# Zero fills in the plan, another order of first loads, V stores by token and three new constants in a kernel whose whole instruction order is planned ahead

## The chip, the cores and the metric

The kernel runs on one core of a Trainium2 chip. The metric is the device time of one execution in microseconds (us), median of several runs. The profile's span is about 1.8 us shorter than the time of the same execution, so spans are compared with spans and times with times.

PE is the matmul engine, DVE the vector engine, ACT the scalar engine, POOL is GpSimd, and SP is the engine that issues most transfers.

## The reference

Two rounds of an attention layer with a recurrent memory, each followed by a gated feed-forward layer, on x of 1 x 2048 x 512 in bf16. What matters is the recurrence: the 2048 tokens go through the attention in 64 segments of 32, and each needs the 8 memory rows that the one before has made.

```python
def _A_ref(x, mem0, Wq, Wk, Wv, Wo, seg_len):          # seg_len 32, 32 heads of 128, M = 8
    ...
    for s in range(n_seg):                             # 64 segments
        h = jnp.concatenate([mem, x[:, s*32:(s+1)*32, :]], axis=1)      # 8 + 32 rows
        q, k, v = (einsum('btd,dhe->bhte', h, W) for W in (Wq, Wk, Wv))
        p = softmax(where(mask, einsum('bhqe,bhke->bhqk', q, k) * scale, -1e9))
        o = einsum('bhte,hed->btd', einsum('bhqk,bhke->bhqe', p, v), Wo)
        mem = o[:, :M, :]                              # on to the next segment
        outs.append(o[:, M:, :])
...
x = x + _A_ref(_layernorm(x), ...);  x = x + _B_ref(_layernorm(x), ...)
x = x + _A_ref(_layernorm(x), ...);  x = x + _B_ref(_layernorm(x), ...)
```

(The einsums are condensed; `_B_ref` is the gated feed-forward layer.)

## The kernel before

Both attention layers run interleaved, the second six segments behind the first. There are thus 70 steps: six with the first layer alone, 58 with both, six with the second alone. V of the x rows does not depend on the recurrence, so it is projected ahead ("V passes") and stored in a DRAM scratch array `scr`; V of the memory rows ("strips") is made in each step. The feed-forward matmuls fill the gaps on PE.

No engine decides at run time. A planner in Python holds a list of tasks with an assumed duration and assumed delays, simulates the engines, and then emits every engine's instructions in the simulated order. Two of its beliefs matter here: the delay between a task and its reader, and how long an SP transfer takes to land, since the planner lets only eight be under way.

```python
class Planner:
    LAT = {"PE": 205.0, "DVE": 110.0, "ACT": 128.0, "POOL": 40.0, "SP": 4000.0}    # ns
    TO_PE = 32.0
    def gap(self, a, b):                               # delay from task a to its reader b
        if a.eng == b.eng:
            return a.lat if a.eng[0] in ("DVE", "ACT", "SP") or len(a.eng) > 1 else 0.0
        return a.lat + (self.TO_PE if b.eng[0] == "PE" else 0.0)
    def forward(self):
        ...                                            # by priority, each engine in turn
                if e == "SP":
                    lanes.append(end + tk.land)        # tk.land: 3000 ns unless set
                    if len(lanes) >= 8:
                        free[e] = max(end, lanes[-8])

def setup_consts(self):                                # emitted first, outside the plan
    identf = fview(self.st[1][:, 0, 0:1], [(1, P)])
    cmasks.make_identity(nc, identf)                   # GpSimd, f32
    nc.vector.tensor_copy(out=self.ident[:], in_=identf)      # cast to bf16
    ...                                                # masks
    for t_ in self.hT: nc.vector.memset(t_[:, :, L:2 * L], 0.0)
    for t_ in self.pb: nc.vector.memset(t_[:], 0.0)
    for k, t_ in enumerate(self.vsb):                  # 5 tiles of 128 x 1024 bf16
        self.pl.add("POOL", 950, lambda t_=t_: nc.gpsimd.memset(t_[:], 0.0), w=[...])

def take_v(self, pst, B, j, tile, keys, c0, r0, n):    # transposed rows into xvf / xvl
    dst = fview(tile[:, 0, c0:c0 + 1], [(P, self.DC), (n, BLK), (1, n)])
    self.pl.add(("ACT", "DVE"), copy_ns(16 * n, True), ...)

def v_pass(...):                                       # V of x rows, then the store
    ...
    d = self.scr[j][...].rearrange("(i r) e -> i r e", i=BLK)[:, r0:r0 + n, :]
    tk = pl.add(("SP", "POOL") if boot else "SP", ..., ("dma", d, vs[c0:c0 + BLK * n, ...]))
    if n == 8:
        tk.land = 8000.0                               # believed: lands after 8 us

def add_strips(col, lo, key):                          # V of the memory rows, two banks
    pl.add("PE", ..., strips, w=vb, ...)
    for q in range(2):
        pl.add(("ACT", "DVE"), copy_ns(512), lambda q=q: (sb[:, q, :], vb[q][:, :]), ...)
    ...                                                # DMA sst -> vsb
...
# end of a step: WO's result; DVE takes the memory rows, ACT the others
pl.add("DVE", 140, lambda: nc.vector.tensor_copy(out=nslot[:, :, SEG:SEG+2*MEM], in_=wo3(SEG, 2*MEM)), ...)
pl.add("ACT", 160, lambda dst=dst, a=48*j - c0: (dst, wo3(a, SEG)), ..., w=[("oxT", ...)])
```

## Time and profile before

| quantity | before | how to read it |
|---|---|---|
| time | 1872.53 us, median of 4 (1869.12 to 1873.32) | the metric |
| busy | PE 97%, DVE 69%, ACT 61%, GpSimd 31% | PE is the bound |
| first V matmul | 11.65 us | end of the start |
| 7th step mark | 223.75 us | see below |
| 64th step mark | 1720.03 us | see below |
| span | 1869.7 us | the profiled execution |

The prediction shows most of the views. I add one kind of line: the DVE copies that hand the memory rows from one segment to the next (the last `tensor_copy` in the code above) happen once a step in every version of the kernel and lie on the recurrence. They are therefore marks at which two kernels can be compared. The timeline of the kernel before has these for the 7th step (the first with both layers) and the 64th (start in us, duration, engine, line, operation, tiles, and in brackets the idle time before it with what ended it):

```profile
223.75 0.23 DVE L824 CAST hT<-bank 128x64 bf16<-128x64 f32 x1 [4.48 <-PE bank L811]
...
1720.03 0.19 DVE L829 CAST hT<-bank 128x32 bf16<-128x32 f32 x1 [0.38 <-PE bank L811]
```

They cut the run into an early part (to 223.75), a middle (1720.03 - 223.75 = 1496.28 us) and a tail (1869.7 - 1720.03 = 149.7 us). One window of the trace (busy us of PE, PEld, DVE, ACT and POOL with counts, then granted clock, DMA share, GB/s):

```profile
130.00:150.00 20.00, 19.05 (x536) 16.52 (x534) 11.24 (x39) 10.49 (x33) 5.18 (x8) 0.83 0.50 145
```

### The profile page before, as it was taken

The numbers are of one execution on the slowest core, as the hardware profiler recorded it, in microseconds if no ns is written. First come the engines' busy times: TensorE is split into PE (matmuls) and PEld (weight loads), VectorE is DVE, ScalarE is ACT, GpSimd is POOL, SyncE is SP. The second block draws the span as 40 slices with busy tenths as digits, with TensorE's granted clock in tenths as the row PEclk, the third lists the DMA queues.
The fourth block names the chain that finished last, engine by engine and source line by source line (L and its number), as shares of the span: only waits on it lengthen the run. The fifth ranks groups of instructions, "written<-read, shape, count | busy, mean of one in ns | idle before, by whom it ended". The sixth has DMA issues, their size and how long they took to land.

```text
span 1869.7 us, 94235 instructions
## 1 busy us (share of the span) xinstructions
PE 1822.6 (97%) x41068; PEld 1577.4 (84%) x41282; DVE 1282.3 (69%) x4167; ACT 1137.3 (61%) x2692; POOL 583.2 (31%) x832
## 2 busy tenths in 40 slices
PE   7999999999999999999999999999999999999999
PEld 3578788888989898989988898989889898988787
DVE  5366577776777667776677677666777677766565
ACT  4655556666666666566666666666666666666554
POOL 5412012332423232333323233233323232333323
PEclk9999999999999999999999999999999999999999
DMA  9733334554645544555545554555545454455534
GB/s 354 247 102 103 89 86 119 153 155 129 182 124 153 151 143 124 151 151 149 166 128 152 147 143 131 141 152 153 157 121 152 136 156 122 141 152 145 158 100 138
DMA packets 130060, 273.83 MB, mean 146 GB/s; under 512 B 29254, under 2 KB 60750, under 8 KB 129646
## 3 DMA queue, kind: packets, MB, share of 16 engines
q0 software_dynamic: 59984, 184.49, 33.7%
q1 hardware_dynamic: 69662, 83.30, 15.5%
q8 instruction: 323, 5.29, 1.2%
q14 instruction: 91, 0.75, 0.1%
HBM read 221.85 MB, written 27.26 MB: 133 GB/s over the span
## 4 chain that ended last, share of the span: by engine, by line
PE 92%; DVE 4%; ACT 2%; issue 1%; DMA 0%; POOL 0%; SPq 0%; ACTq 0%; DVEq 0%; POOLq 0%
PE bank L708 32%; PE bank L811 16%; PE bank L910 11%; PE bank L570 9%; PE bank L680 7%; PE bank L722 5%; PE bank L781 4%; PE bank L794 4%; PE bank L934 4%; PE bank L540 1%; DVE st L735 1%; ACT otsb L1002 1%; DVE pb L764 0%; DMA vsb<-sst 0%; PE bank L878 0%
## 5 line engine op out<-in xcount | busy, mean ns | idle before, releaser
L708 PE MATMUL bank<-hT,wq_sb 128*128 128x80 bf16 (+1 forms) x8960 | 624.2, 198 | 5.7 <-issue 1.7
L708 PE MATMUL bank<-hT,wk_sb 128*128 128x80 bf16 (+1 forms) x8960 | 622.9, 198 | 1.4 <-issue 1.4
L1002 ACT CAST qku<-bank 128x480 bf16<-128x480 f32 (+3 forms) x770 | 393.9, 512 | 265.5 <-PE bank L708 253.3
L708 PEld LDWEIGHTS <-wq_sb 128*128 128x128 bf16 x8960 | 458.1, 99 | 27.9 <-issue 8.5
L708 PEld LDWEIGHTS <-wk_sb 128*128 128x128 bf16 x8960 | 450.7, 99 | 1.6 <-issue 1.6
L735 DVE TENSOR_TENSOR st<-bank,maskb 80x240 f32<-80x240 f32 (+1 forms) x732 | 268.7, 368 | 234.5 <-PE bank L722 227.7
L811 PE MATMUL bank<-otsb,wo_sb 128*128 128x80 bf16 (+1 forms) x8960 | 371.8, 198 | 7.4 <-ACT otsb L1002 5.5
L811 PEld LDWEIGHTS <-wo_sb 128*128 128x128 bf16 x8960 | 339.7, 99 | 21.5 <-issue 10.3
L902 POOL DMA_DIRECT2D wg<-in_B_w_gate_dram x217 | 165.0, 760 | 489.4 <-PE bank L910 419.7
L1002 ACT CAST otsb<-bank 128x480 bf16<-128x480 f32 (+3 forms) x420 | 200.8, 486 | 76.7 <-PE bank L794 61.9
L928 POOL DMA_DIRECT2D wd<-in_B_w_down_dram x217 | 153.7, 710 | 256.6 <-PE bank L794 98.5
L764 DVE TENSOR_TENSOR pb<-st,rz 80x480 bf16<-80x480 f32 x348 | 205.8, 592 | 3.5
L745 ACT ACTIVATE st<-st 80x240 f32<-80x240 f32 (+3 forms) x420 | 159.8, 382 | 64.6 <-DVE st L742 62.7
L1002 ACT CAST ptsb<-bank 128x480 bf16<-128x480 f32 (+3 forms) x315 | 155.3, 499 | 65.2 <-PE bank L781 62.9
L530 POOL TENSOR_TENSOR lns<-lns,negh 128x1 f32<-128x1 f32 (+1 forms) x79 | 45.4, 576 | 449.0 <-DVE lns L529 334.7
L722 PE MATMUL bank<-qku 128*80 128x80 bf16 (+1 forms) x2240 | 176.7, 202 | 1.8 <-ACT qku L1002 0.4
L747 DVE TENSOR_REDUCE sm<-st 80x6 f32<-80x240 f32 (+3 forms) x420 | 151.7, 362 | 35.5 <-ACT st L745 33.4
L910 PE MATMUL bank<-xnT,wg 128*128 128x128 bf16 (+2 forms) x1784 | 171.8, 219 | 1.5 <-ACT xnT L1002 0.2
L910 PE MATMUL bank<-xnT,wu 128*128 128x128 bf16 (+2 forms) x1784 | 171.2, 218 | 0.1
L722 PEld LDWEIGHTS <-qku 128*80 128x80 bf16 (+1 forms) x2240 | 129.9, 117 | 46.2 <-issue 11.5
L903 POOL DMA_DIRECT2D wu<-in_B_w_up_dram x217 | 162.5, 749 | 4.6 <-PE bank L781 1.4
L742 DVE TENSOR_TENSOR st<-st,mx 80x240 f32<-80x240 f32 (+3 forms) x420 | 155.7, 371 | 3.9
(98 smaller groups left out, 2475.1 us busy)
## 6 DMA issues: line engine op xcount, KB each, us to landing
wg<-in_B_w_gate_dram POOLq DMA_DIRECT2D x220, 256.0 KB, 4.3
wu<-in_B_w_up_dram POOLq DMA_DIRECT2D x220, 256.0 KB, 4.7
wd<-in_B_w_down_dram POOLq DMA_DIRECT2D x220, 256.0 KB, 5.2
vsb<-scr SPq DMA_DIRECT2D x508, 48.0 KB
vsb<-sst SPq DMA_DIRECT2D x280, 64.0 KB
scr<-vst SPq DMA_DIRECT2D x128, 96.0 KB
wv_sb<-in_A_Wv_dram SPq DMA_DIRECT2D x4, 1024.0 KB
wq_sb<-in_A_Wq_dram SPq DMA_DIRECT2D x5, 768.0 KB
```

Source lines behind the costliest of these rows:

```text
L570: nc.tensor.matmul(B[:, :], lhsT=tile[:, c, :], rhs=self.wv[:, c, cs], start=(c == 0), stop=(c == DC - 1))
L708: nc.tensor.matmul(o_ap, lhsT=W[:, c, h * P:(h + 1) * P], rhs=mv(c), start=(c == 0), stop=(c == DC - 1))
L722: nc.tensor.matmul(s_all(SB)[pr, uh - h0 + i, :], lhsT=qku[:, i, 0, 0:ncol], rhs=qku[:, i, 1, 0:ncol], start=True, stop=True)
L735: pl.add("DVE", dve_ns(n, True), lambda gsz=gsz, hs=hs, st=st, SB=SB, pj_=pj_, npj_=npj_, mk=mk, idx=idx: nc.vector.tensor_tensor(out=st[p ...
L742: pl.add("DVE", dve_ns(n), lambda gsz=gsz, hs=hs, st=st, mx=mx: nc.vector.tensor_tensor(out=st[pr, hs], in0=st[pr, hs], in1=mx[pr, hs].uns ...
L745: pl.add("ACT", act_ns(n), lambda hs=hs, st=st: nc.scalar.activation(out=st[pr, hs], in_=st[pr, hs], func=ACTF.Exp, scale=self.scale), r=s ...
L764: nc.vector.tensor_tensor(out=o, in0=st[pr, hs].unsqueeze(1).to_broadcast([npart, 2, gsz, L]), in1=rz[pr, :, 0:gsz].unsqueeze(3).to_broadc ...
L811: nc.tensor.matmul(WB[:, c * ncol:(c + 1) * ncol], lhsT=self.wo[:, h, c * P:(c + 1) * P], rhs=otsb[:, hl, 0:ncol], start=(h == 0 and c == ...
L902: pl.add("POOL", 760, lambda wg=wg, fs=fs: nc.gpsimd.dma_start(out=wg[:], in_=self.wgv[:, :, fs]), r=[("wo", self.H - 1)], w=[gk] + bt, la ...
L903: pl.add("POOL", 760, lambda wu=wu, fs=fs: nc.gpsimd.dma_start(out=wu[:], in_=self.wuv[:, :, fs]), r=[("wo", self.H - 1)], w=[uk] + bt, la ...
L910: nc.tensor.matmul(gu[:, 2 * i + k, 0:n], lhsT=W[:, c, i * P:(i + 1) * P], rhs=xnT[:, c, rw], start=(c == 0), stop=(c == DC - 1))
L1002: nc.scalar.copy(out=dst, in_=src)
```

## The change

The intent is to start PE sooner, to store V with more DMA engines at once, and to tell the planner more exactly when three results are ready. In its four parts:

1. **Start.** The identity is built in bf16 with no cast; the `vsb` fills leave GpSimd (one on DVE, four as ACT copies), fills become planned tasks; x blocks are loaded ahead of V weights and `mem0` after them.
2. **Layout of V stores.** The rows of a store that holds part of a block are ordered by token instead of by segment.
3. **Belief about these stores.** The 8000 ns landing time of 8-token stores is dropped, so the planner assumes the ordinary 3000.
4. **Three constants** `late`: the strips' first bank is believed ready 980 ns sooner, qku's source 40 ns later, oxT's source 240 ns later.

```diff
+        if late:                                      # in Planner.add
+            tk.adj = {d: late for d in tk.fresh if self.tasks[d].eng == ("PE",)}
 ...
-        return a.lat + (self.TO_PE if b.eng[0] == "PE" else 0.0)
+        return a.lat + d + (self.TO_PE if b.eng[0] == "PE" else 0.0)
 ...
-        identf = fview(self.st[1][:, 0, 0:1], [(1, P)])
-        cmasks.make_identity(nc, identf)
-        nc.vector.tensor_copy(out=self.ident[:], in_=identf)
+        cmasks.make_identity(nc, self.ident[:])
 ...
-            self.pl.add("POOL", 950, lambda t_=t_: nc.gpsimd.memset(t_[:], 0.0), w=[...])
+            if k == 0:
+                pl.add("DVE", 550, lambda t_=t_: nc.vector.memset(t_[:], 0.0), w=keys)
+            else:
+                pl.add("ACT", 960, lambda t_=t_: nc.scalar.copy(out=t_[:], in_=self.vsb[0][:]), r=[("vs", 0)], w=keys)
 ...
-        for h0 in range(0, self.H, 8):                # V weights in pieces of 8 heads
+        for h0, n in ((0, 4), (4, 4), (8, 8), (16, 8), (24, 8)):
 ...
-        dst = fview(tile[:, 0, c0:c0 + 1], [(P, self.DC), (n, BLK), (1, n)])
+        dst = fview(tile[:, 0, c0:c0 + 1], [(P, self.DC)] + ([(n, BLK), (1, n)] if n == XS else [(1, BLK), (BLK, n)]))
 ...
-                d = self.scr[j][...].rearrange("(i r) e -> i r e", i=BLK)[:, r0:r0 + n, :]
+                d = self.scr[j][...]
+                if n < XS:
+                    d = d.rearrange("(i r) e -> r i e", i=BLK)[r0:r0 + n]
 ...
-                if n == 8:
-                    tk.land = 8000.0
 ...
-   pl.add(("ACT", "DVE"), copy_ns(512), ..., w=[(sb, q)], use=[sb])
+   pl.add(("ACT", "DVE"), copy_ns(512), ..., w=[(sb, q)], use=[sb], late=-980.0 * (q == 0))
-   pl.add("ACT", act_ns(2 * nh * ncol, True), qkcopy, r=[pq], w=[qku])
+   pl.add("ACT", act_ns(2 * nh * ncol, True), qkcopy, r=[pq], w=[qku], late=40.0)
-   pl.add("ACT", 160, ..., w=[("oxT", j, oi, s % BLK)])
+   pl.add("ACT", 160, ..., w=[("oxT", j, oi, s % BLK)], late=240.0)
```

(Cut: the bookkeeping of `adj`, the fills of `hT` and `pb` as tasks, the move of x block 2 and `mem0`, assumed rates and delays of some loads.)

## The prediction

> **What bounds the kernel now.** I read the page's busy shares first, then the chain that ended last, then a table of busy time by stage, then what the matmul engine (PE) waits for, and last the timeline of the first 20 us.
>
> ```profile
> PE 1822.6 (97%) x41068; PEld 1577.4 (84%) x41282; DVE 1282.3 (69%) x4167; ACT 1137.3 (61%) x2692; POOL 583.2 (31%) x832
> PE 92%; DVE 4%; ACT 2%; issue 1%; DMA 0%; POOL 0%; SPq 0%; ACTq 0%; DVEq 0%; POOLq 0%
> ```
>
> Both say that this is a kernel bound by PE. The others have room, and 92% of the chain is matmuls. The change removes no matmul: the instruction order of the built program has 41,282 weight loads and as many matmuls on PE before and after. So all it can win is time in which PE stood still or ran slowly. The table by stage (window, then the busy us of PE, PEld, DVE, ACT, POOL with counts, then clock, DMA share, GB/s) tells where that time lies:
>
> ```profile
> 0.00:20.00 20.00, 9.28 (x45) 4.33 (x46) 14.26 (x49) 6.41 (x15) 10.86 (x26) 1.00 0.92 318
> 20.00:120.00 100.00, 98.87 (x1589) 62.08 (x1600) 44.76 (x136) 61.07 (x139) 40.23 (x69) 1.00 0.70 232
> 120.00:320.00 200.00, 190.33 (x4571) 162.57 (x4585) 134.95 (x442) 119.17 (x301) 41.48 (x58) 0.98 0.38 107
> 320.00:1700.00 1380.00, 1360.99 (x30767) 1213.53 (x30935) 980.95 (x3188) 864.78 (x1990) 436.37 (x606) 1.00 0.51 145
> 1700.00:1870.00 170.00, 163.15 (x4111) 134.89 (x4122) 107.40 (x355) 85.84 (x249) 54.24 (x75) 1.00 0.48 136
> ```
>
> Window less PE busy: 10.7 us idle in the first 20 us, 1.1 in the next 100, 9.7 up to 320, 19.0 in the long steady stage (1.4% of it) and 6.9 at the end, 47.4 us in all. This is the whole purse, 2.5% of the span. A fall of over 2%, 37.4 us, would need four fifths of it.
>
> The waits of PE over the whole span (what waited, for what: us in total, times, longest), and the timeline of the start:
>
> ```profile
> PE bank L513 <- DVE ident L451: 6.4, 1, 6.4
> PE bank L811 <- ACT otsb L1002: 5.5, 19, 0.7
> PE bank L540 <- DVE xn L531: 4.8, 5, 2.8
> PE bank L794 <- DMA vsb<-sst: 1.5, 3, 0.9
> ...
> 3.00 3.38 DVE L451 CAST ident<-st 128x128 bf16<-128x128 f32 x1
> 3.57 2.73 POOL L471 MEMSET vsb<- 128x1024 bf16 x3
> 6.81 1.28 DVE L527 BATCH_NORM_STATS2 lns<-xs 128x6 f32<-128x512 bf16 x2
> 11.65 3.60 PE L570 MATMUL bank<-wv_sb,xvf 128*128 128x512 bf16 x8 [0.36 <-ACT xvf L1002]
> 16.20 2.76 PE L570 MATMUL bank<-wv_sb,xvf 128*128 128x512 bf16 x12 [0.53 <-ACT xvf L1002]
> ```
>
> The reader is to see one chain here. The cast of the identity holds DVE from 3.00 to 6.38 us. DVE works in order, so the statistics of the first x block start only at 6.81, and the first projection of V at 11.65, 4.84 us later.
>
> **What the Trainium skill says.** (1) "SBUF — State Buffer", section "Who interferes with whom": a DVE copy or cast in a 2-port mode and a GpSimd instruction exclude each other for the whole instruction. The trace agrees: the cast ends at 6.38, 0.08 us after GpSimd's last fill of vsb (3.57 + 2.73 = 6.30), though casting 128 elements a partition elsewhere on DVE takes about 0.2 us. (2) "TensorE: Matmul & The Clock Gate", Part 1: a cold array runs at half clock, 426.7 ns for a matmul of 512 columns against 215.7 warm. The trace agrees: 8 in 3.60 us are 450 ns each, 12 in 2.76 us 230 each. (3) "DMA: Bandwidth & Descriptors", section "Why a DMA increments its semaphore by 16 and not by 1": the number of DMA engines is the largest number up to 16 that divides the slowest dimension of both sides. A store written 4x16 gets 4 engines and 16x4 gets 16. The trace leans that way: the list of DMA issues has 128 KB boot stores (4x16) landing after 6.2 to 7.1 us, but 192 KB ones (96 rows) after 5.9 to 6.3. (4) "VectorE: DVE Perf Modes", section "Zero memsets can be issued as uint32": the fill takes a cycle per element, so half as many 4-byte elements take half the time. The trace has three such fills of 384 elements in 1.19 us, 0.40 each.
>
> **The change part by part.**
>
> *Identity and fills.* GpSimd now builds the bf16 identity first: one fill and one select, which took 0.20 and 0.29 us before; no cast is left. GpSimd's five fills of vsb (0.94 us each) become one DVE fill and four ACT copies. In the new order DVE has five tiny fills (done by about 1.2 us), three of pb (1.19), one of vsb (512 elements, an estimate of 512/384 x 0.40 = 0.53) and eight of hT (0.7), then the statistics: 1.2 + 1.2 + 0.5 + 0.7 = 3.6 us, say 3.7. The x block must have landed. It is now the first transfer issued, at about 0.75 us; the 8 KB mem0 landed 1.64 us after its issue, so for 128 KB I estimate 2.5 us, landing at 3.2. Then the statistics start at 3.7 in place of 6.81: **3.1 us sooner**. The same 4.84 us of layernorm, transposes and copies follows, so the first V matmul starts at about 8.5.
>
> The catch is ACT. Its four copies of vsb take an estimated 1.03 us each (0.59 for 512 elements of bf16 in the trace, plus 512 x 0.85 ns), so from 3.0 they end at 7.1. ACT's first copy of a transpose is wanted at 3.7 + (10.15 - 6.81) = 7.0. That is a tie: I take off 0.1 us. Gain: 3.0.
>
> *Order of the first loads.* x block 2 goes ahead of the V weights and mem0 behind it; the first V weight piece is halved. This attacks the next hole: between 11.65 and 19.02 PE did 20 V matmuls (8 cold at 450, 12 at 230: 6.4 us) and stood for about 0.9 us before 16.20 for a copy of block 2. I expect half of it back, 0.5 us. The V weights cannot become the bound: the first half MB needs to land by 8.5 us, and at the 380 GB/s of this stage the 0.9 MB ahead of and with it take 2.4 us, from 2 us on. From 20 to 120 us PE is 99% busy although DMA is saturated until 68 us, as it has V projections to fill in; so a start 3 us earlier carries through. Sum of the start: **-3.5 us**.
>
> *V stores by token.* Same bytes, more engines per store. The only waits for stores are ACT's in the first 80 us, about 1.8 us in total; PE has none. By itself: 0. Indirectly the plan no longer believes in a slow landing (8 us) of the 8-token stores, and orders the SP queue anew.
>
> *Plan.* Three constants: the strips' first bank 980 ns sooner, qku 40 ns and oxT 240 ns later. They cost no instruction; they reorder ACT and DVE. In the order of the built program all but 14 of the 142 sst copies are now on ACT (86 before), which relieves DVE of 42 x 0.68 = 29 us and loads ACT with 42 x 0.585 = 25 us; and before oxT, where ACT stood idle 57.7 us in all for the hT copy of the same bank, it now finds work in 23 steps (30 before), but more of it. What PE can win: part of 4.7 us for otsb and 1.2 us for the strips' rows (its waits between 150 and 1800 us), and part of many gaps under 0.3 us. I count a third of the 35.6 us of idle after 120 us as movable by order, and a third of that won: about **-4 us**. One stretch more is at stake: between 130 and 150 us the granted clock is 0.83, so 20 x 0.17 = 3.4 us are lost to a cold array after a string of waits. An order with fewer waits there may avoid it, another may fall into it twice: **-0.5** on average.
>
> Sum: -3.5 - 4 - 0.5 = -8. 1872.3 - 8 = **1864 us**, 0.4% faster.
>
> **The rivals.** *Start alone:* the order in the steady stage was good already (98.6% busy), and the reordering gives and takes as much. Then 1868.8. For it: PE's waits there are short and scattered, and ACT gets the sst copies just where PE waits for ACT. *The plan bites:* a plan closer to the chip removes most of the waits for ACT and the cold stretch: -3.5 - 9 - 3.4 = 1856. For it: 120 to 320 us holds 9.7 us of idle in a seventh of the time of the steady stage, where chains of waits are seen and one event cures several. *A wait takes the place of the one removed:* ACT's fills run late, x lands at 4.5 us, or the weights arrive later, as the first pieces are small, and half of the start's gain goes; with a worse steady stage by 2 us, 1872. Against it: 1.2 us of slack at landing, and DMA at 0.78 of its time in the first 10 us. *ACT becomes the bound* of the steady stage through 25 us more: not believable at 61%, and the shifts of ptsb and xnT copies to DVE weigh against it.
>
> **Range and chances.** The start is near sure (-2.5 to -4), the plan uncertain (-10 to +4), the cold stretch a coin (3.4 us). That makes 1856 to 1871. The runs of before spread over 4.2 us. Over 2% faster (below 1834.8) would need nearly all idle time: 0.01. Over 2% slower has no cause in sight: 0.005. Within: 0.985.
>
> **What would show it.** Right: in the new timeline no DVE instruction of over 1 us before the statistics, which start at 3.5 to 4.0 us; first V matmul between 8.2 and 9.0; PE idle in the first 20 us near 7.5 (10.7 before); PE's wait for the identity gone; ACT's idle before oxT below 50 us; idle after 120 us at 28 to 34 us (35.6). Wrong: PE's first V matmul waits for a DMA of x or of the V weights, or for ACT's fills; a new stretch of granted clock under 1; the steady stage's PE idle at or over 19.0, which would leave the start alone.

## The result, and the profile after

The changed kernel takes **1861.33 us**, median of 4 runs (1858.97 to 1861.92), against 1872.53 us before: a ratio of 0.9941, with a 95% interval of 0.9924 to 0.9959. A ratio here is the mean time of one kernel's fast runs over that of the other's in the same rounds, so it is not quite the ratio of the medians. The time lies in the range, in the class "within 2%", and 2.7 us below the number predicted.

The page of the changed kernel has its busy shares, and the chain that ended last, as follows:

```profile
PE 1818.1 (98%) x41066; PEld 1577.1 (85%) x41282; DVE 1274.6 (69%) x4115; ACT 1173.8 (63%) x2748; POOL 571.8 (31%) x821
PE 94%; DVE 2%; ACT 2%; issue 1%; DMA 1%; POOL 0%; SPq 0%; ACTq 0%; DVEq 0%; POOLq 0%
```

The picture is the same: PE is the bound as before, the 41,282 weight loads are the same, and ACT with 36.5 us more work has gone from 61% to 63%. The time came out of gaps. The table by stage, with the columns as above:

```profile
0.00:20.00 20.00, 10.77 (x56) 5.00 (x58) 12.33 (x50) 11.34 (x20) 8.38 (x24) 1.00 0.91 313
...
120.00:320.00 200.00, 192.27 (x4545) 163.58 (x4565) 130.53 (x428) 123.92 (x303) 46.51 (x67) 1.00 0.40 113
320.00:1700.00 1380.00, 1365.57 (x30941) 1218.93 (x31104) 991.08 (x3181) 894.03 (x2038) 436.98 (x607) 1.00 0.51 146
1700.00:1859.10 159.10, 150.71 (x3775) 124.93 (x3783) 91.16 (x301) 80.29 (x238) 50.01 (x70) 0.96 0.47 134
```

Two clocks changed: 0.98 has become 1.00 between 120 and 320 us, and 1.00 has become 0.96 at the end. The timeline of the changed kernel shows the start, and the two step marks:

```profile
2.42 0.48 DVE L479 MEMSET vsb<- 128x512 uint32 x1
2.94 3.88 ACT L481 COPY vsb<-vsb 128x1024 bf16<-128x1024 bf16 x4 [0.92 <-DVE vsb L479]
3.66 1.29 DVE L539 BATCH_NORM_STATS2 lns<-xs 128x6 f32<-128x512 bf16 x2
8.75 0.72 DVE L1019 COPY xvf<-bank 128x256 bf16<-128x256 bf16 x1 [0.61 <-ACT xvf L1017]
8.77 1.89 PE L583 MATMUL bank<-wv_sb,xvf 128*128 128x512 bf16 x4 [0.62 <-ACT xvf L1017]
...
217.23 0.22 DVE L837 CAST hT<-bank 128x64 bf16<-128x64 f32 x1 [5.12 <-PE bank L824]
...
1705.93 0.19 DVE L842 CAST hT<-bank 128x32 bf16<-128x32 f32 x1 [1.92 <-PE bank L824]
```

The cast is gone, the statistics follow the fills with no wait, and the first V matmul comes at 8.77 us in place of 11.65. The marks say where the whole gain lies: the 7th step comes 223.75 - 217.23 = 6.5 us sooner; the middle takes 1705.93 - 217.23 = 1488.7 us, 7.6 less; the tail takes 1859.1 - 1705.9 = 153.2 us, 3.5 more. Together -6.5 - 7.6 + 3.5 = **-10.6 us** of span.

What PE waits for, over the whole span of the changed kernel (us in total, times, longest):

```profile
PE bank L552 <- DVE xn L543: 5.0, 5, 2.1
PE bank L525 <- DMA xo<-in_A_mem_dram: 4.0, 1, 4.0
PE bank L824 <- ACT otsb L1017: 3.7, 8, 0.7
PE bank L807 <- DMA vsb<-sst: 3.0, 5, 1.4
```

The wait of 6.4 us for the identity has gone; a wait of 4.0 us for `mem0` stands there, but PE's first V matmul was released by ACT's copy (the bracket at 8.77), so `mem0` is not what set the start. The waits for otsb fell from 5.5 to 3.7 us; those for the strips' rows rose from 1.5 to 3.0.

### The profile page after: what moved, and what is told of

The parts are those of the page before. It is cut to its first block, busy times and chain, and to the rows that moved or that the text cites. A ratio compares the mean times of both kernels' runs of the same rounds, so it can differ in the third digit from the quotient of the medians.

```text
span 1859.1 us, 94041 instructions
## 1 busy us (share of the span) xinstructions
PE 1818.1 (98%) x41066; PEld 1577.1 (85%) x41282; DVE 1274.6 (69%) x4115; ACT 1173.8 (63%) x2748; POOL 571.8 (31%) x821
## 4 chain that ended last, share of the span: by engine, by line
PE 94%; DVE 2%; ACT 2%; issue 1%; DMA 1%; POOL 0%; SPq 0%; ACTq 0%; DVEq 0%; POOLq 0%
PE bank L721 33%; PE bank L824 16%; PE bank L923 11%; PE bank L583 9%; PE bank L693 7%; PE bank L735 5%; PE bank L794 4%; PE bank L807 4%; PE bank L947 4%; PE bank L552 1%; DMA vsb<-sst 0%; PE bank L891 0%; ACT otsb L1017 0%; ACT ptsb L1017 0%; DVE ptsb L1019 0%
## 5 line engine op out<-in xcount | busy, mean ns | idle before, releaser
L824 PE MATMUL bank<-otsb,wo_sb 128*128 128x80 bf16 (+1 forms) x8960 | 368.0, 198 | 7.0 <-ACT otsb L1017 3.7
L735 PE MATMUL bank<-qku 128*80 128x80 bf16 (+1 forms) x2240 | 163.0, 202 | 1.4 <-ACT qku L1017 0.3
L735 PEld LDWEIGHTS <-qku 128*80 128x80 bf16 (+1 forms) x2240 | 123.6, 117 | 42.0 <-ACT sst L1017 22.1
```

What stands on the lines that cost most here:

```text
L735: nc.tensor.matmul(s_all(SB)[pr, uh - h0 + i, :], lhsT=qku[:, i, 0, 0:ncol], rhs=qku[:, i, 1, 0:ncol], start=True, stop=True)
L824: nc.tensor.matmul(WB[:, c * ncol:(c + 1) * ncol], lhsT=self.wo[:, h, c * P:(c + 1) * P], rhs=otsb[:, hl, 0:ncol], start=(h == 0 and c == ...
```

## The experiments

A few microseconds are asked about, and one change of order can move as much. So all kernels but g3 ran 3 rounds beside the kernel before, on the same chip, and g3 had one look. For each I give the median, the ratio, and three readings of its profile against the profile of before: the lead at the 7th step mark, the length of the middle, and the us that the trace's clock records show at half clock between 100 and 320 us. This "cold" time always came in multiples of 3.41 us. Each of these three readings is of one execution, and the clock varies between executions of one kernel: the 28 runs of the kernel before had mean clocks from 0.995 to 1.000.

The middle and the marks are used in place of PE's idle time for a reason that experiment f1 shows.

| label | what ran | time, us | ratio (95%) | 7th step | middle | cold 100-320 |
|---|---|---|---|---|---|---|
| | after | 1861.33 | 0.9941 (0.9924-0.9959) | -6.5 | -7.6 | 0 (before: 6.8) |
| e1_start_only | part 1 alone | 1868.64 | 0.9975 (0.996-0.999) | -3.1 | -1.4 | 0 |
| e2_token_only | parts 2, 3 alone | 1870.74 | 0.9986 (0.9971-1.0001) | +5.4 | -6.3 | 17.1 |
| e3_late_only | part 4 alone | 1870.58 | 0.9986 (0.9969-1.0002) | 0.0 | -3.3 | 3.4 |
| e4_sham_before | before, one constant 1 ns off | 1871.15 | 0.9987 (0.9972-1.0002) | +0.5 | -0.8 | 6.8 |
| f1_land_only | part 3 alone | 1868.25 | 0.9976 (0.9962-0.9991) | +2.7 | -6.3 | 13.7 |
| f2_token_keepland | part 2 alone | 1881.07 | 1.0047 (1.003-1.0064) | +6.3 | +0.9 | 10.2 |
| f3_after_nolate | parts 1, 2, 3 | 1869.56 | 0.998 (0.9965-0.9995) | +5.3 | -7.2 | 13.7 |
| f4_after_notoken | parts 1, 4 | 1866.61 | 0.9974 (0.9958-0.999) | -3.1 | -4.3 | 0 |
| g1_after_landonly | parts 1, 3, 4 | 1858.74 | 0.9934 (0.9915-0.9952) | -3.5 | -10.2 | 3.4 |
| g2_sham_after | after, one constant 1 ns off | 1857.35 | 0.9919 (0.9905-0.9934) | -5.3 | -10.6 | 0 |
| g3_ident_only | identity without cast alone | 1871.41, one run | none | -2.7 | +0.8 | 3.4 |
| h1_strip_const | after, only the strips' constant of part 4 | 1862.57 | 0.9938 (0.9916-0.996) | -4.1 | -6.5 | 3.4 |

The kernel before had medians of 1873.95 (e1 to e4), 1873.01 (f1 to f4), 1872.52 (g1 to g3) and 1873.11 us (h1).

Two things about the cold time can be worked out from these traces. The first is what it costs. Matmuls of 40 columns (the free size of their result) follow one another every 25 ns at full clock and every 33 at half clock, those of 80 columns every 36 and 67 (medians over all traces). Counted in this way, matmul by matmul, the cold stretch of before cost an estimated 1.3 us, as all its recorded matmuls have 40 columns; those of f1, f3 and e2 between 100 and 320 us cost 4.6, 5.6 and 5.7, and those in the tail of the changed kernel 4.0.

The second is what comes before it. The clock records of a trace change on a grid of 3.41 us. If all 14 traces are cut into windows on this grid, without the last 4 us, 38 windows at full clock are followed by half clock. In each of them the matmuls streamed at most 3,508 columns, and of the 7,486 other windows at full clock only 6 streamed as few. PE's busy time does not separate them: the 38 have 1.28 to 3.31 us of it, and 722 of the others have no more than 3.31. So a window can be nearly full of short matmuls and still be the one before a cold stretch, as at 138.6 us in the kernel before (3.26 us busy, 3,499 columns). No run changed the columns alone, so this is a regularity of the traces and not a cause that was tried.

### The start: e1 and g3

e1 takes the kernel before and makes part 1 alone:

```diff
-        cmasks.make_identity(nc, identf); nc.vector.tensor_copy(out=self.ident[:], in_=identf)
+        cmasks.make_identity(nc, self.ident[:])
+        ...  fills on DVE and ACT, x block 2 first, V weights in a half piece first, mem0 behind
```

> The kernel before with the change's start alone: identity without a cast, zero fills planned on DVE and ACT, x block 2 first, mem0 after it, first V weight piece halved. No new constants for lateness, V stores as before. Theory (each part adds its own gain): the first V matmul starts near 8.8 us as in the changed kernel (11.65 before), 3 to 4 us are kept to the end, so about 1868.5 and a ratio of 0.998. Rival (the parts only work together, as the planner draws a new order each time): the gain at the end is anywhere between +4 and -10 us whatever the start gains, and the time of the last steps does not follow from the 3 us of the start.

Its first V matmul starts at 8.60 us, its 7th step comes 3.1 us sooner, and its time is 0.9975 of before. The start carries through to the recurrence at nearly the size of the prediction's sum for it (-3.5 us), as its theory had it (about 1868.5 us). But e1 also lacks the cold stretch of before, an estimated 1.3 us of the 3.1, so one profile does not settle what the start alone is worth there to better than that, nor the 0.5 us that should have come from block 2.

g3 keeps the order of every instruction of the kernel before, GpSimd's fills too, and takes the cast away alone:

```diff
-        identf = fview(self.st[1][:, 0, 0:1], [(1, P)])
-        cmasks.make_identity(nc, identf)
-        nc.vector.tensor_copy(out=self.ident[:], in_=identf)
+        cmasks.make_identity(nc, self.ident[:])
```

> The kernel before with the identity built in bf16 on GpSimd, so without the cast; GpSimd's five fills of vsb stay. One look at the start. Theory (the cast waits for GpSimd's fills, and only a two-port instruction of DVE does): DVE's statistics start at 3.2 to 3.7 us in place of 6.81, but the power of the variance on GpSimd now waits for the fills to end at about 6.1 us, so the first V matmul comes at about 9.5 to 10.0 (8.77 in the changed kernel, 11.65 before). Rival (x lands late, the cast hid it): statistics not before 5 us.

Its timeline:

```profile
3.35 1.29 DVE L525 BATCH_NORM_STATS2 lns<-xs 128x6 f32<-128x512 bf16 x2 [0.18 <-DMA xs<-in_A_x_dram]
3.57 2.73 POOL L469 MEMSET vsb<- 128x1024 bf16 x3
6.28 1.08 POOL L528 TENSOR_TENSOR lns<-lns,negh 128x1 f32<-128x1 f32 x2
9.49 3.60 PE L568 MATMUL bank<-wv_sb,xvf 128*128 128x512 bf16 x8 [0.36 <-ACT xvf L1000]
```

GpSimd's fills run at the same 3.57 us for the same 2.73 us as before, yet DVE's statistics are no longer held up: they start at 3.35 in place of 6.81, as soon as x has landed. So it was the cast that was held up while GpSimd filled, not DVE as such; that the fills held it is read from the 0.08 us between their ends in the trace of before, as no run moved the fills alone. The layernorm then waits a second time, because its power runs on GpSimd behind the fills (6.28). That leaves the first V matmul at 9.49, and the rest of part 1 (the fills moved off GpSimd and the order of loads, not taken apart) is worth the remaining 9.49 - 8.60 = 0.9 us. The lead at the 7th step is 2.7 us. This run is a single one of unknown state; it is used for its start alone.

### V stores: f1, f2, e2 and g1

The prediction gave the V stores nothing by themselves. e2 makes the whole change to them alone, that is the layout and the belief together:

```diff
-        dst = fview(tile[:, 0, c0:c0 + 1], [(P, self.DC), (n, BLK), (1, n)])
+        dst = fview(tile[:, 0, c0:c0 + 1], [(P, self.DC)] + ([(n, BLK), (1, n)] if n == XS else [(1, BLK), (BLK, n)]))
...
+                if n < XS: d = d.rearrange("(i r) e -> r i e", i=BLK)[r0:r0 + n]
-                if n == 8: tk.land = 8000.0
```

> The kernel before with V stored by token alone (and the planner's belief in an 8 us landing of the 8-token stores gone). Theory: stores cost PE nothing, so the ratio is 1.000, within 0.1%. Rival A: in the boot stage the stores on few DMA engines hold back the first steps, and the first step's memory copy (89.7 us before, 76.7 in the changed kernel) moves by several us; ratio 0.997. Rival B (any change draws a new order): -5 to +5 us, without a cause in the stores.

The time is hardly moved (0.9986), but the stages are: 5.4 us later at the 7th step, 6.3 us shorter in the middle. Something is gained and something lost. f1 and f2 make the two halves of it separately. f1 drops the belief and keeps the old layout:

```diff
-                tk = pl.add(...)
+                pl.add(...)
-                if n == 8:
-                    tk.land = 8000.0
```

> The plan's belief alone: the kernel before, its V stores unchanged (4x8 and 4x16 shapes), but the planner no longer believes that an 8-token store takes 8 us to land. Its instruction order is the same as that of the run with V stored by token, only the shape of the stores differs. Theory (the belief draws a better order): PE's idle in the steady stage (320 to 1700 us) falls from 19.0 to about 12.4 us as in that run, ratio near 0.9986. Rival (the shape matters, more DMA engines for a store): idle in the steady stage stays near 19 or grows, as rows are now wanted before slow stores have landed, and waits for a DMA of scr appear in PE's list.

f2 takes the new layout and keeps the belief:

```diff
+        dst = ... [(1, BLK), (BLK, n)]
+                if n < XS: d = d.rearrange("(i r) e -> r i e", i=BLK)[r0:r0 + n]
                 if n == 8: tk.land = 8000.0
```

> The shape of the stores alone: V stored by token, the belief of an 8 us landing kept, so the instruction order is exactly that of the kernel before. Theory: nothing moves, ratio 1.000 within 0.1%, steady idle near 19 us, the first step's copy near 89.7 us. Rival (the shape matters): SP's waits for the landing of stores (20.3 us in the steady stage before) fall and the time falls by 3 us or more.

The layout does not enter the plan, so f2 has the order of before, and e2 the order of f1. These two pairs show the layout by itself, and in these two orders it **costs**: f2 is at 1.0047 of before, by far the slowest kernel, with its 7th step 6.3 us later; e2 reaches its 7th step 5.4 - 2.7 = 2.6 us later than f1 (unrounded 5.37 - 2.73), with a middle equal to the hundredth (1489.99 us in both), though the ratios of e2 and f1 (0.9986 and 0.9976) have intervals that overlap. Both theories for the layout, "nothing moves", failed. The groups of instructions by form say why (line, engine, operation, tiles, shapes, count, then busy us and mean ns). In f1:

```profile
L1000 ACT COPY xvf<-bank 128x256 bf16<-128x256 bf16 x5 | 1.7, 376 | 0.9 <-PE bank L570 0.9
L1002 DVE COPY xvf<-bank 128x256 bf16<-128x256 bf16 x1 | 0.3, 291 | 0.0
```

and in e2:

```profile
L1002 ACT COPY xvf<-bank 128x256 bf16<-128x256 bf16 x5 | 3.3, 769 | 0.8 <-PE bank L570 0.8
L1004 DVE COPY xvf<-bank 128x256 bf16<-128x256 bf16 x1 | 0.7, 722 | 0.2 <-ACT xvf L1002 0.2
```

The same copy of the same 256 elements takes 769 in place of 376 ns on ACT and 722 in place of 291 on DVE. What differs is the destination: the rows of a store come from the columns of `xvf`, so ordering them by token makes the copy that fills `xvf` write every fourth element. The Trainium skill, "VectorE: DVE Perf Modes", section "What auto-detection actually checks", has the fast 16-bit mode only where every tensor has step 1. The trace agrees with a loss of that mode and goes beyond it: the 128-element copies on DVE take 224 ns in the old layout and 444 in the new, so an element costs (291 - 224)/128 = 0.52 ns before and (722 - 444)/128 = 2.17 ns after, four times as much rather than twice.

These copies stand ahead of the V matmuls with which PE fills the first 120 us. In f2 the array also warms up later: its clock records have full clock from 20.7 us on (from 15.7 before), and the second batch of V matmuls, 2.76 us long in the timeline of before, is

```profile
16.83 4.67 PE L570 MATMUL bank<-wv_sb,xvf 128*128 128x512 bf16 x12 [0.81 <-ACT xvf L1004]
```

These 4.67 - 2.76 = 1.9 us are not shown to be the layout's: e2, with the same copies, was at full clock from 14.7 us. At the mark of the first step e2 is 1.5 us behind f1 (90.99 against 89.49), and f2 is 3.4 us behind before (93.12 against 89.74), so 1.5 us without the late warm-up. What is added up to the 7th step is in good part more cold time (an estimated 1.1 us between e2 and f1, 2.0 between f2 and before).

The stores themselves do land sooner by token. In the list of DMA issues (KB each, median us from issue to landing), before:

```profile
scr<-wg POOLq DMA_DIRECT2D x10, 128.0 KB, 7.1
```

and f2, in the same order (the changed kernel has 5.5):

```profile
scr<-wg POOLq DMA_DIRECT2D x10, 128.0 KB, 5.7
```

So the part does what it intends, 1.4 us a store, in a place where PE waited for no store.

The **belief** is the half that wins. The marks of f1 are

```profile
226.48 0.23 DVE L822 CAST hT<-bank 128x64 bf16<-128x64 f32 x1 [6.73 <-PE bank L809]
...
1716.46 0.19 DVE L827 CAST hT<-bank 128x32 bf16<-128x32 f32 x1 [0.83 <-PE bank L809]
```

The middle of the run is shorter by 6.3 to 10.6 us in all seven profiles that have part 3 (after, e2, f1, f3, g1, g2, h1; five instruction orders), and differs by -4.3 to +0.9 us in the six others (five orders with that of before). The stores are the same whatever the planner believes; what changes is the order. By the planner's code, a belief of 8 us keeps its eight lanes full for longer and holds SP back in the plan. How long these stores really take in the middle is in no view that I read (the boot stores above took 5.5 to 7.1 us in three kernels), so the route from the belief to the shorter middle is read from the code and not shown step by step. What the trace shows is the end of it: what PE waits for in the steady stage sums to 2.7 us in f1 and to 9.7 before. As missing records can look like waits, compare the five traces that have all: 2.7 to 3.2 us with the new belief (f1, f3, h1), 7.8 and 11.1 with the old (f4, f2).

How not to read this is instructive. The windows of f1 and of e2 for the steady stage:

```profile
320.00:1700.00 1380.00, 1375.52 (x31069) 1218.73 (x31067) 1001.99 (x3222) 869.14 (x1995) 442.63 (x607) 1.00 0.51 145
```

```profile
320.00:1700.00 1380.00, 1367.65 (x30944) 1219.45 (x31092) 1002.43 (x3222) 871.53 (x1995) 443.18 (x607) 1.00 0.50 145
```

PE seems idle for 4.5 us in f1 and for 12.4 in e2. But both have one order and one middle, and f1 has 125 matmul records more in this window: f1's trace has all of the program's 41,282, e2's only 41,085. The idle 7.9 us are mostly records that are missing. The trace of before lacks 214 records as well.

g1 asks about the layout once more, inside the changed kernel: same order as after, old layout, new belief.

```diff
-        dst = ... ([(n, BLK), (1, n)] if n == XS else [(1, BLK), (BLK, n)])
+        dst = fview(tile[:, 0, c0:c0 + 1], [(P, self.DC), (n, BLK), (1, n)])
-                d = ...; if n < XS: d = d.rearrange("(i r) e -> r i e", i=BLK)[r0:r0 + n]
+                d = self.scr[j][...].rearrange("(i r) e -> i r e", i=BLK)[:, r0:r0 + n, :]
```

> The changed kernel with its instruction order kept, but the V stores and the copies that feed them back in the old layout (4x8 and 4x16 stores). Alone, the layout by token cost 2.5 us between two kernels of one order, as its copies into xvf write every fourth element (719 for 291 ns on DVE, 771 for 376 on ACT). Theory (the layout is a loss, the planner's belief the gain): faster than the changed kernel by 1 to 3 us, about 1858.5 to 1860.5, ratio 0.9925 to 0.9935. Rival (in this order the shape of the stores is needed, rows are fetched before slow stores land): 1863 or more, with waits for a DMA of scr in PE's or SP's list.

It runs in 1858.74 us, 0.9934 of before, which is the number of its theory. But in this order the layout is not clearly a loss: with it the first step's mark comes 2.4 us sooner (76.68 against 79.10) and the 7th 3.0 us sooner, while the middle and the tail are 2.6 and 2.5 us longer, and the two ratios (0.9941 and 0.9934) have intervals that overlap widely. So the layout costs where it was tried in the two other orders; what it does in the changed kernel's own order is not settled.

### The constants, and what they need: e3, e4, f3, f4, h1

e3 takes part 4 alone:

```diff
+ ... late=-980.0 * (q == 0)      # strips' first bank
+ ... late=40.0                   # qku
+ ... late=240.0                  # oxT
```

> The kernel before with the three constants of lateness alone (strips' first bank 980 ns sooner, qku 40 ns and oxT 240 ns later). Theory: the steady stage and the single-layer stages win some 4 to 8 us, seen as a lead that grows step by step from 320 to 1700 us; ratio 0.997, start unchanged (first V matmul near 11.65). Rival (the start alone carries the gain): ratio 1.000.

e4 is its control. It changes the plan by a constant that can mean nothing, and so shows what a new order is worth by luck:

```diff
-                pl.add("ACT", act_ns(2 * nh * ncol, True), qkcopy, r=[pq], w=[qku])
+                pl.add("ACT", act_ns(2 * nh * ncol, True), qkcopy, r=[pq], w=[qku], late=1.0)
```

> A sham: the kernel before with qku believed 1 ns later in the plan, which means nothing on the chip but lets the planner draw a new order. It measures how much a new order alone moves the time. Theory (the constants of the change work by what they say): within 0.1% of the kernel before, 1871 to 1874. Rival (luck of the draw): it moves by 3 us or more, either way, which is as much as the parts of the change.

Both give the same ratio, 0.9986 and 0.9987, and both intervals end just above 1. Alone, the three constants cannot be told from a constant of one nanosecond; e3's theory (0.997) and its rival (1.000) are both inside its interval.

f3 and f4 take one part out of the changed kernel each. f3 has no constants:

```diff
-  ... late=-980.0 * (q == 0))      -  ... late=40.0)      -  ... late=240.0)
+  ... )                            +  ... )               +  ... )
```

> The changed kernel without the three constants of lateness: start and V stores stay. Theory (the constants are worth about as much as alone, 2 to 3 us): 1863 to 1865, ratio 0.995 to 0.996. Rival (the parts need each other, the constants make up the missing 4 us): 1866 to 1868, near the run of the start alone.

f4 has the old V stores, layout and belief:

```diff
+        dst = fview(tile[:, 0, c0:c0 + 1], [(P, self.DC), (n, BLK), (1, n)])
+                if n == 8:
+                    tk.land = 8000.0
```

> The changed kernel with the old V stores and the old belief in an 8 us landing: start and constants stay. Theory (the belief wins about 6 us in the steady stage): about 1866 to 1867, ratio 0.997, idle from 320 to 1700 us near 18 (14.4 in the changed kernel). Rival (the constants alone win in the steady stage): 1862, ratio 0.9945, idle near 14.

With the start in all kernels of the table:

| with the start | old belief (8 us) | new belief (3 us) |
|---|---|---|
| no constants | 0.9975 (e1) | 0.998 (f3, new layout) |
| constants | 0.9974 (f4) | 0.9934 (g1, old layout), 0.9941 (after, new layout) |

On top of the start, neither the constants alone (e1 to f4) nor the belief alone (e1 to f3) show a gain, with intervals of about 0.15% either way. f3's theory (1863 to 1865 us) failed and its rival, that the parts need each other (1866 to 1868), came nearest to the 1869.56 measured; f4's theory (1866 to 1867) held with 1866.61. **Together the two are worth 0.3 to 0.4%**, some 6 to 7.5 us, more than the start's 0.25%. The four kernels with both (after, g1, g2, h1) lie at 0.9919 to 0.9941, and of the kernels without both none is below 0.9974.

That the two *need* each other is less well shown. On the kernel before, the belief did win alone (0.9976, f1), f3 bears the new layout besides, and the start with the new belief in the old layout was not run. And the rival that the parts simply add up fits the finished kernels: start, belief and constants alone give 0.9975 x 0.9976 x 0.9986 = 0.9937 (g1: 0.9934), and with e2 in place of f1 0.9947 (after: 0.9941). Against it speak only f3 and f4, for which the parts would give 0.9961 each; they fall short of that by 0.0019 and 0.0013, no more than the 0.0022 that one nanosecond moves below (g2). So the gain of all parts together is measured, and how it divides between belief and constants is open.

The stages say what stands between f3 and the changed kernel: f3 has the short middle that comes with the belief (-7.2 us), but reaches its 7th step 5.3 us *later* than before in spite of a start that was 2.9 us sooner. The clock window of f3 between 190 and 210 us:

```profile
190.00:210.00 20.00, 17.89 (x410) 16.30 (x408) 10.86 (x34) 9.50 (x23) 3.88 (x6) 0.83 0.29 86
```

and of the changed kernel:

```profile
190.00:210.00 20.00, 18.77 (x348) 13.16 (x347) 14.87 (x50) 13.59 (x28) 0.00 (x0) 1.00 0.16 41
```

All three kernels with the belief but no strips' constant (e2, f1, f3) lie cold for 13.7 to 17.1 us between 100 and 320 us; all four with both (after, g1, g2, h1) for 0 to 3.4. All their runs agree with these single profiles: the mean clock of the whole span is 0.9952 over the 12 runs of the three, and 0.9971 over the 16 runs of the four. In f3 these 13.7 us cost an estimated 5.6, about half of the 11.8 us between f3 and the changed kernel at the 7th step. The Trainium skill, "TensorE: Matmul & The Clock Gate", section "A second HAM failure mode: psum-queue depth-cycling", tells of a matmul engine that idles briefly often enough for its clock to oscillate. The traces here agree with that in part only: the clock does fall and return in stretches of 3.41 us, but what marks the windows before is few columns, with or without idle time (1.28 to 3.31 us busy).

h1 asks which of the three constants it takes, and keeps the strips' one:

```diff
-                pl.add("ACT", act_ns(2 * nh * ncol, True), qkcopy, r=[pq], w=[qku], late=40.0)
+                pl.add("ACT", act_ns(2 * nh * ncol, True), qkcopy, r=[pq], w=[qku])
-            pl.add("ACT", 160, ..., late=240.0)
+            pl.add("ACT", 160, ...)
```

> The changed kernel with the strips' constant (first bank 980 ns sooner) as its only constant of lateness; qku and oxT are planned as before. Without any of the three the time was 1869.6, as cold stretches of the clock came back between 150 and 230 us. Theory (the strips' constant is the one that counts, it is by far the largest and moves the strips' copies to ACT): 1858 to 1863, ratio 0.992 to 0.995, no or one cold stretch between 100 and 320 us, and 7 to 11 us won between the 7th and the 64th step. Rival (the small constants of qku and oxT carry it): 1866 to 1870 and several cold stretches there, as without any constant.

It is enough: 1862.57 us, 0.9938, 3.4 us cold, as its theory had it (the middle won 6.5 us, just short of the 7 to 11 forecast). The other two constants, 40 and 240 ns, are not needed for the gain. The three windows ahead of f3's cold stretches streamed 1,434, 2,707 and 2,422 columns, while no window of the changed kernel between 100 and 320 us streamed fewer than 4,128. By what steps an earlier belief about the strips spreads the matmuls so is **not shown**; an order of tens of thousands of instructions changes in too many places, and this stays open.

### Luck of the order: g2

g2 is the control on the other side, the changed kernel with 41 ns in place of 40:

```diff
-                pl.add("ACT", act_ns(2 * nh * ncol, True), qkcopy, r=[pq], w=[qku], late=40.0)
+                pl.add("ACT", act_ns(2 * nh * ncol, True), qkcopy, r=[pq], w=[qku], late=41.0)
```

> A sham on the changed kernel: qku believed 41 ns later in place of 40. It measures how far its time rests on the one order that the planner happened to draw. Theory (the constants work by what they say): 1860 to 1863, ratio 0.9935 to 0.995. Rival (a lucky order): 1864 to 1870, with cold stretches of the clock between 130 and 250 us that the changed kernel does not have.

It is the fastest kernel, 1857.35 us (1856.86 to 1858.14), a ratio of 0.9919, and beats both kernels. It lies outside its theory and its rival, on the fast side. It has no idea that the changed kernel lacks. Its middle is 3.1 us shorter and its tail 151.3 us in place of 153.2, with 3.4 us of cold clock there in place of 13.7. So up to 4.0 us between medians (with ratio intervals that just overlap) come out of one nanosecond in a belief: differences of this size between two orders prove nothing about their ideas. The end of the run shows the same in all profiles: tails of 149.7 us with no cold clock, of 149.9 to 151.3 with 3.4 us of it, of 150.7 to 151.8 with 6.8, of 151.6 to 152.8 with 10.2, and 153.2 with 13.7.

## Why the prediction was right or wrong

The time was right, with a sum of -8 against -11.2 us measured in medians. Its parts were not all right, step by step:

**Identity and fills: right.** Statistics at 3.66 us (3.7 predicted), first V matmul at 8.77 (8.5); g3 shows that DVE is not held up once the cast is gone. (The trace has no cast of 128 elements besides, as the prediction reads it; those of 80 take 0.24 us and those of 160 take 0.32.) The tie on ACT did not occur: each copy of `vsb` takes 1.04 us as estimated, but the four overlap at their ends and take 3.88 together, not 4.1, so they ended at 6.82, ahead of the 7.0 at which they were in the way. The V matmul's other 0.17 us are the token layout, which the working left out: with the old layout (e1, f4, g1) it starts at 8.60.

**Order of the first loads: wrong in size.** "I expect half of it back, 0.5 us" is not seen: e1's lead at the 7th step is 3.1 us, no more than that of its first V matmul. PE was idle for 20 - 10.77 = 9.2 us of the first 20, not 7.5; in the changed kernel it waits 1.6 us for a layernorm at 16 us, where before it waited for a copy.

**"V stores by token. ... By itself: 0": the step that failed most.** It looked at who waits for a store and not at who makes its rows. The copies of 256 elements became 2.0 to 2.5 times as long. By the first step this cost 1.5 us in two orders (f2 without its late warm-up), and by the 7th the kernels were 2.6 us (e2 against f1) and 6.3 us behind (f2 against before), cold time included. In the changed kernel's own order no cost was settled. The sentence after it, on the 8 us that the plan no longer believes in, named a part of the real gain but gave it no number.

**"Plan. Three constants ... about -4 us": the size nearly right, the cause wrong.** Measured from the 7th step's 3.1 us of the start, the plan won 6.5 - 3.1 = 3.4 us early and 7.6 in the middle and gave 3.5 back at the end: -7.5, against -4.5 with the cold stretch. But the three constants alone do what a sham does (e3, e4), and on top of the start they add nothing that shows (f4). The gain past the start was measured with the belief and the strips' constant together, and the prediction gave the belief no number; how much is due to each is open.

**The cold stretch "a coin": right in kind, wrong in size.** The stretch of 6.8 us near 140 us went, and 13.7 us of cold clock appeared in the tail. The first had cost an estimated 1.3 us, not 3.4, as matmuls of 40 columns lose 8 of 33 ns and not half; the second cost an estimated 4.0, enough for the 3.5 us by which the tail is longer. "A new stretch of granted clock under 1" was among the prediction's own signs of being wrong, and it came. The rival "the plan bites" (1856) thus came out early and in the middle, and lost some of it at the end. The rival "start alone" (1868.8) is the measurement of e1 (1868.64) and f4 (1866.61): it was the right reading of a change with the constants but not the belief. Of "a wait takes the place of the one removed" only the 4.0 us for `mem0` came, and they did not set the start.

**The purse of 47.4 us: overstated.** It took PE's idle time as read. The trace of before lacks 214 matmul records, and f2, of the same order and with all its records, has 12.2 us of idle time in the steady stage in place of 19.0.

**Checks.** Held: no long DVE instruction ahead of the statistics; the wait for the identity gone; idle after 120 us 7.7 + 14.4 + 8.4 = 30.6 us (28 to 34). Missed: ACT's idle before oxT should have fallen below 50 us and rose from 57.7 to 62.1, as the group shows:

```profile
L1017 ACT CAST oxT<-bank 128x128 bf16<-128x128 f32 x128 | 28.5, 270 | 62.1 <-DVE hT L837 53.6 <-DVE hT L842 8.5
```

So the reordering ahead of oxT did not do what it was read to do, and h1 has its gain without oxT's constant.

## What to carry to other kernels

In a kernel whose order is planned ahead, a change of layout is also a change of the copies that make the layout: look for the stride of their writes before counting what the transfer saves. Beliefs of the planner may act in company, so take each out of the finished kernel as well as putting it alone into the old one, and run a sham of one nanosecond on both sides to know what luck is worth. Compare stages by marks that every version has, since idle time of the bound engine depends on which records the trace kept. Where the clock falls with PE nearly always busy, count the columns that its matmuls stream, not its busy time.

## What the Trainium skill lacked or had wrong

- **Copies with a strided 16-bit destination**, "VectorE: DVE Perf Modes" and, for ACT, "ScalarE: Activation LUTs". Writing every fourth bf16 element from PSUM to SBUF cost 2.17 ns an element on DVE against 0.52, more than the loss of the two-elements mode that the first page has, and (769 - 441)/128 = 2.6 ns on ACT against (376 - 265)/128 = 0.9. The note on cache lines in "SBUF — State Buffer", section "Door 1: The DMA port swizzle", lets 8 bf16 elements be strided for free; a stride of 4 was not free here.
- **How full a window keeps the array warm**, "TensorE: Matmul & The Clock Gate". The page ties the return to half clock to an idle window, and has one case of brief idling. Here PE was busy for 19.05 of 20 us (before, 130 to 150 us) and for 17.89 (f3, 190 to 210 us) at a mean clock of 0.83, but for 18.77 at 1.00 (after, 190 to 210 us). Busy share does not tell which window falls cold; columns streamed in 3.41 us nearly do (at most 3,508 in all 38 windows before half clock, as few in 6 of 7,486 others), and the page gives no such measure.
- **Matmul records that are missing**, "Perfetto Trace Analysis", section "Identifying the Most-Contended Engine". It warns of matmul busy time for another reason. Two traces of one order had 41,282 and 41,085 records and differed by 7.9 us in PE's busy time over the steady stage, with a middle of 1489.99 us in both.
